# Rounding angles straight from PSUM, with ScalarE emptying the products and taking the absolute value

## The chip, the cores and the metric

The kernel runs on one core of a Trainium2 chip. A core has TensorE (PE in the profile, its weight loads PEld), VectorE (DVE), ScalarE (ACT), GpSimd (POOL) and SyncE (SP, which only issues transfers). The metric is the device time of one launch in microseconds. The kernel before took 1151.37, 1149.21 and 1151.18 us in three runs (median 1151.18).

## The reference

For 8 batches with 8 heads, 576 rows and head size 64, float32: scores scaled by 1/sqrt(64); those more than `tau` = 0.02 under the row's largest are dropped; softmax; product with v. The heads of a batch side by side give x (576 × 512). Then a mixture with trigonometric weights:

```
theta = x @ w_theta
zr, zi = x * cos(theta), x * sin(theta)
y = w_tok_r @ zr + w_tok_i @ zi          (over the 576 rows)
u = x + y
out = u + max(u @ w_ch, 0)
```

The change lies in how cos(theta) and sin(theta) are formed.

## The kernel before, in words

**Attention.** Heads go in pairs, four pairs to a batch, 32 in all. A pair has nine blocks of scores (128 query rows of one head, the last one 64 rows of both). For each: scores on PE into PSUM (L278); L282 on VectorE copies them negated to SBUF and takes the row minimum; L295 adds `tau`; L299 on ScalarE is the exp; L300 on VectorE masks and sums. Four transposes (L326) and a fifth (L341) follow on PE, and ScalarE copies their results to SBUF (L331, L333 for the last block, L344, L348). When the first 256 query columns are there, and again after the other 320, the value product o_ps (L361, 20 matmuls) runs, and L362 on ScalarE copies it out. L377 to L386 normalise.

**The mixture.** `moe(b)` handles batch b while the attention of batch b + 1 runs. Its operands are transposed: 4 chunks m of 128 of the 512 columns, each 128 partitions × 576. For each m:

- *angle*: 24 matmuls give the product in two halves of 288 columns, each in a PSUM buffer (m_ps, L405). The half is emptied into `th` as turns (angle / 2 pi), by ScalarE for m = 0 and 1 (L444), by VectorE for m = 2 and 3 (L446). Adding and subtracting the constant `MAGIC` rounds to whole turns (L453, SBUF to SBUF, into `km`); L454 takes the difference, a fraction between −1/2 and 1/2.
- *sines*, for two m at a time: L463 on VectorE clears the sign bit into the first half of `z`; ScalarE loads the Sin table (L467), makes the cosine from the absolute value (L471) and the sine from the fraction (L472), and loads the Exp table again (L476). GpSimd multiplies both with x (L483); in the last batch VectorE does.
- *flip*: z is transposed (z_ps, L495), copied out in a high part by ScalarE (L497) and a low part by VectorE (L498).
- *token*: 54 matmuls per m (y_ps, L512), added to x by L515. At the end comes the product with w_ch, L560.

**What sets the order.** PE's order is written by hand: `fill()` lets the mixture yield pieces between the blocks of attention, and `ORDER = "a0 a1 s01 a2 a3f0 s23 t0f1 t1f2 t2f3 t3"` sets the mixture's steps (a angle, s sines, f flip, t token). On the other engines a scheduler with its own time model orders the instructions at compile time, by priorities: attention's are raised by `ATTENTION` (20), the sines and the table loads by `SINES` (10000). `after(...)` adds order without a semaphore. So the order on VectorE, ScalarE, GpSimd and SP's queue can change wherever an instruction of the mixture changes.

**Buffers.** Six PSUM buffers (`ps_t`) are shared by m_ps, z_ps, y_ps, t_ps, o_ps and those of normalising; a buffer comes free when all readers of its content are done. Four SBUF buffers (`temp`, tag t576) are shared by `th`, `km`, the reciprocal rows `rb`, and the raw q and k that SP loads (`qraw`, `kraw`) and from which ScalarE and GpSimd prepare the next pair (L100, L109, L225, L226, L228). Three buffers hold `z`.

Of the kernel before, what the change touches and what calls it, by code (L numbers as in the profile page):

```python
# [12 lines left out]
U32 = mybir.dt.uint32  # L13
AF = mybir.ActivationFunctionType
ALU = mybir.AluOpType
# [3 lines left out]
MAGIC = 12582912.0  # L19
TURN = 2.0 * math.pi  # L20

TURN_IN = 6.283185
# [17 lines left out]
def tile_attn_moe(  # L40
# [11 lines left out]
    nc = tc.nc  # L52
    B, NP, D, _, S = qT.shape
# [3 lines left out]
    HS = S // 2  # L57
# [53 lines left out]
    def temp(name, dt=F32):  # L111
        return pool.tile([P, S], dt, tag="t576", name=name, bufs=4)

    def after(ins, other):

        info = mybir.DependencyInfo(mybir.DependencyClass.NoSync, mybir.DependencyReason.DATA)
        tc.add_manual_dep(ins.ins, other.ins.name, info, reason="order")
        return ins
# [71 lines left out]
    def get_wm(which, m):  # L190
        t = pool.tile([P, 2, NM, P], F32R, tag="wm", name=f"wm{which}", bufs=3)
        nc.gpsimd.dma_start(t, wm_dram[which, m].bitcast(F32R))  # L192
        return t
# [234 lines left out]
    def moe(b):  # L428
# [7 lines left out]

        def angle(m):
            th = temp("th")
            wm = get_wm(0, m)

            def evict(ps, hs):

                if m < 2:
                    nc.scalar.activation(out=th[:, hs], in_=ps[:, :HS], func=AF.Copy, scale=1.0 / TURN)  # L444
                else:
                    nc.vector.tensor_scalar(  # L446
                        out=th[:, hs], in0=ps[:, :HS], scalar1=1.0 / TURN, scalar2=None, op0=ALU.mult
                    )

            yield from product(wm, xs, evict, m == 0)  # L450

            km = temp("km")
            nc.vector.tensor_scalar(out=km, in0=th, scalar1=MAGIC, scalar2=-MAGIC, op0=ALU.add, op1=ALU.add)  # L453
            nc.vector.tensor_tensor(out=th, in0=th, in1=km, op=ALU.subtract)  # L454
            zs[m, "f"] = th

        def sines(ms):

            todo = []
            for m in ms:  # L460
                th = zs.pop((m, "f"))
                z = pool.tile([P, 2 * S], F32, tag="z", name="z", bufs=3)
                ab = nc.vector.tensor_scalar(  # L463
                    out=z[:, :S].bitcast(U32), in0=th.bitcast(U32), scalar1=0x7FFFFFFF, scalar2=None, op0=ALU.bitwise_and
                )
                todo.append((m, th, z))
            ahead_of = after(nc.scalar.preload_act_table(AF.Sin), ab)  # L467
            with tc.high_priority(offset=SINES):
                for m, th, z in todo:
                    ins = [  # L470
                        nc.scalar.activation(out=z[:, :S], in_=z[:, :S], func=AF.Sin, scale=-TURN_IN, bias=half_pi),  # L471
                        nc.scalar.activation(out=z[:, S:], in_=th, func=AF.Sin, scale=TURN_IN),  # L472
                    ]
                    for x in ins:
                        after(x, ahead_of)
                exp = nc.scalar.preload_act_table(AF.Exp)  # L476
                for x in ins:
                    after(exp, x)
            for m, th, z in todo:
                x = xT[b * NP + m]  # L480
                for i in range(2):
                    zi = z[:, i * S : i * S + S]
                    lo_eng.tensor_tensor(out=zi, in0=zi, in1=x, op=ALU.mult)  # L483
                zs[m] = z
# [41 lines left out]
        for what in ORDER.split():  # L526
            ms = [int(x) for x in what if x.isdigit()]
            turns = what[2:3] == "f"
            what, m = what[0], ms[0]
            if what == "a":  # L530
                other = flip(ms[1]) if turns else iter(())
                for n, cost in enumerate(angle(m)):
                    yield cost
                    if n > 1:
                        yield next(other, 0)
                for cost in other:
                    yield cost
                left -= 1
            elif what == "s":
                sines(ms)  # L540
            elif what == "f":
                yield from flip(m)
            else:
                other = flip(ms[1]) if turns else iter(())
                for n, cost in enumerate(token(m)):
                    yield cost
                    if n % 5 == 2:
                        yield next(other, 0)
                for cost in other:
                    yield cost  # L550
                done.append(m)
            while left == 0 and done:
                split_u(done.pop(0))
# [146 lines left out]
```

## Time and profile before

| | |
|---|---|
| three runs, us | 1149.21, 1151.18, 1151.37 |
| profiled execution: span, us (the page gives no other time for it) | 1147.4 |
| busy us: PE / PEld | 1043.9 / 921.5 |
| busy us: DVE / ACT / POOL | 869.0 / 750.0 / 375.1 |
| chain that ended last: PE / DVE / ACT | 64% / 15% / 13% |

The profile is that of one execution. A row of groups gives line, engine, operation, output <- inputs, shapes and count, then after the bar the busy time in us and the mean of one in ns, and then the idle time of that engine just before, with what ended it. A row of waits gives engine, tile and line, what it waited for, the sum in us, how often, and the longest. A row of the timeline gives start and duration in us, and in brackets the idle time before it and what ended it; adjacent instructions of one kind are put in one row with their count. A row of windows gives the busy time of each engine in a stretch, then the granted clock of PE as a share of full speed.

### The profile page before, as it was taken

The numbers are of one execution on the slowest core, as the hardware profiler recorded it, in microseconds if no ns is written. First come the engines' busy times: TensorE is split into PE (matmuls) and PEld (weight loads), VectorE is DVE, ScalarE is ACT, GpSimd is POOL, SyncE is SP. The second block draws the span as 40 slices with busy tenths as digits, with TensorE's granted clock in tenths as the row PEclk, the third lists the DMA queues.
The fourth block names the chain that finished last, engine by engine and source line by source line (L and its number), as shares of the span: only waits on it lengthen the run. The fifth ranks groups of instructions, "written<-read, shape, count | busy, mean of one in ns | idle before, by whom it ended". The sixth has DMA issues, their size and how long they took to land.

```text
span 1147.4 us, 21175 instructions
## 1 busy us (share of the span) xinstructions
PE 1043.9 (91%) x7736; PEld 921.5 (80%) x7736; DVE 869.0 (76%) x2139; ACT 750.0 (65%) x1394; POOL 375.1 (33%) x303
## 2 busy tenths in 40 slices
PE   4888888799899998999979998999989999799998
PEld 3566687688779987898869987799878998689898
DVE  7998777987877677876787768776788678787362
ACT  6766869666676566964677666865678656774350
POOL 2203325233342243521443234422435314430210
PEclk9999999999999998999999999999999999999999
DMA  7722223255231052213432142311522133310421
GB/s 252 213 81 84 64 71 97 88 138 148 76 100 53 28 178 74 79 47 103 116 100 63 32 146 76 102 53 34 173 87 72 43 113 104 97 32 1 120 71 60
DMA packets 55176, 105.26 MB, mean 92 GB/s; under 512 B 11936, under 2 KB 20128, under 8 KB 55072
## 3 DMA queue, kind: packets, MB, share of 16 engines
q1 hardware_dynamic: 45856, 70.35, 20.9%
q0 software_dynamic: 9216, 33.56, 10.2%
q8 instruction: 61, 1.00, 0.4%
q14 instruction: 43, 0.35, 0.1%
HBM read 90.24 MB, written 13.63 MB: 91 GB/s over the span
## 4 chain that ended last, share of the span: by engine, by line
PE 64%; DVE 15%; ACT 13%; issue 4%; DMA 2%; POOL 1%; SPq 0%; ACTq 0%; POOLq 0%; DVEq 0%
PE y_ps L512 15%; PE m_ps L405 13%; PE o_ps L361 13%; PE s_ps L278 11%; PE t_ps L326 7%; DVE sc L282 3%; DVE s_sb L300 3%; DVE km L453 3%; ACT s_sb L299 3%; DMA qraw<-in_qT_dram 2%; ACT a L331 2%; PE rb_ps L377 1%; PE z_ps L495 1%; ACT z L471 1%; ACT z L472 1%
## 5 line engine op out<-in xcount | busy, mean ns | idle before, releaser
L300 DVE SCALAR_TENSOR_TENSOR s_sb<-sc,nm,s_sb 128x576 f32<-128x576 f32 x288 | 276.1, 960 | 69.4 <-ACT s_sb L299 65.5
L299 ACT ACTIVATE s_sb<-sc,nm 128x576 f32<-128x576 f32 x288 | 224.1, 778 | 110.8 <-DVE sc L282 109.9
L278 PE MATMUL s_ps<-k,qq 128*128 128x288 f32 (+1 forms) x1344 | 240.2, 307 | 53.8 <-DVE sc L282 39.8
L282 DVE TENSOR_SCALAR_CACHE_REDUCE sc<-s_ps 128x576 f32<-128x576 f32 x288 | 216.7, 753 | 67.2 <-PE s_ps L278 64.3
L278 PEld LDWEIGHTS s_ps<-k,qq 128*128 128x128 f32 x1344 | 193.8, 192 | 81.4 <-DVE sc L282 46.6
L361 PE MATMUL o_ps<-a,v 128*64 128x320 f32 (+1 forms) x1280 | 180.2, 430 | 31.2 <-DVE nm L295 27.7
L331 ACT COPY a<-t_ps 128x512 f32<-128x512 f32 x256 | 148.2, 579 | 58.2 <-PE t_ps L326 56.9
L326 PE MATMUL t_ps<-ident,s_sb 128*128 128x128 f32 x1152 | 175.4, 275 | 1.7 <-DVE zl L498 1.7
L361 PEld LDWEIGHTS o_ps<-a,v 128*64 128x64 f32 x1280 | 92.5, 143 | 97.8 <-ACT s_sb L299 30.4
L512 PE MATMUL y_ps<-wt_h,zh 128*128 128x288 f32 x576 | 165.2, 305 | 6.3 <-DVE zl L498 4.8
L512 PE MATMUL y_ps<-wt_l,zh 128*128 128x288 f32 x576 | 163.0, 301 | 0.0
L109 POOL TENSOR_TENSOR k<-kraw,k 128x576 fp32r<-128x576 f32 x62 | 90.8, 1465 | 202.4 <-ACT k L100 201.0
L228 POOL TENSOR_TENSOR qq<-qraw,qq 64x576 fp32r<-64x576 f32 x62 | 95.1, 1534 | 159.9 <-ACT qq L226 130.4
L326 PEld LDWEIGHTS t_ps<-ident,s_sb 128*128 128x128 f32 x1152 | 142.4, 142 | 3.8 <-DVE zl L498 1.9
L512 PEld LDWEIGHTS y_ps<-wt_h,zh 128*128 128x128 f32 x576 | 108.6, 188 | 8.1 <-DVE zl L498 6.2
L512 PEld LDWEIGHTS y_ps<-wt_l,zh 128*128 128x128 f32 x576 | 108.6, 189 | 0.0
L512 PE MATMUL y_ps<-wt_h,zl 128*128 128x288 f32 x576 | 103.6, 306 | 0.0
L192 POOL DMA_DIRECT2D wm<-wm_dram x64 | 36.4, 570 | 171.0 <-PE m_ps L405 142.6
L405 PE MATMUL m_ps<-xh,wm 128*128 128x288 f32 x512 | 91.5, 305 | 0.3 <-ACT xh L100 0.3
L483 POOL TENSOR_TENSOR z<-z,xT 128x576 f32<-128x576 f32 x56 | 80.0, 1457 | 31.5 <-ACT z L471 31.4
L109 POOL TENSOR_TENSOR ul<-xT,uh 128x576 fp32r<-128x576 f32 x24 | 34.7, 1448 | 169.8 <-DVE uh L104 169.8
L405 PE MATMUL m_ps<-uh,wm 128*128 128x288 f32 x512 | 84.0, 299 | 0.0
(85 smaller groups left out, 1641.9 us busy)
## 6 DMA issues: line engine op xcount, KB each, us to landing
wm<-wm_dram POOLq DMA_DIRECT2D x64, 512.0 KB, 4.0
qraw<-in_qT_dram SPq DMA_DIRECT2D x128, 144.0 KB, 2.9
kraw<-in_kT_dram SPq DMA_DIRECT2D x128, 144.0 KB, 2.9
out_dram<-xT SPq DMA_DIRECT2D x32, 288.0 KB, 2.2
v<-in_vp_dram SPq DMA_DIRECT2D x32, 256.0 KB, 2.7
wraw<-in_w_tok_dram SPq DMA_DIRECT2D x9, 576.0 KB, 5.0
wraw<-in_w_theta_dram SPq DMA_DIRECT2D x4, 512.0 KB, 4.4
wm_dram<-whi SPq DMA_DIRECT2D x8, 256.0 KB, 2.3
```

The lines of the kernel that those rows point to most:

```text
L109: eng_lo.tensor_tensor(out=lo, in0=src, in1=hi.bitcast(F32), op=ALU.subtract)
L228: eng.tensor_tensor(out=qq[64:128], in0=raw[64:128], in1=qq[64:128].bitcast(F32), op=ALU.subtract)
L278: nc.tensor.matmul(ps[:, h, d0:d1], st, kk, start=(x == 0), stop=(x == len(todo) - 1))
L282: nc.vector.tensor_scalar(out=sc.rearrange("p (a b) -> p a b", a=2), in0=ps[:, :, :HS], scalar1=-1.0, scalar2=None, op0=ALU.mult, op1=ALU.min,
L299: nc.scalar.activation(out=e, in_=u.ps[j], func=AF.Exp, bias=nm[:, j : j + 1], scale=-1.0)
L300: nc.vector.scalar_tensor_tensor(out=e, in0=u.ps[j], scalar=nm[:, 2 + j : 3 + j], in1=e, op0=ALU.is_le, op1=ALU.mult, accum_out=u.pr.rows[ ...
L326: nc.tensor.transpose(out=tp[:, c * P : (c + 1) * P], in_=u.sf[:, k0 + c * P : k0 + (c + 1) * P], identity=ident)
L331: nc.scalar.copy(out=t.a[:, :, j, q0 : q0 + P], in_=tp.rearrange("p (c q) -> p c q", c=4))
L361: nc.tensor.matmul(o[64 * j : 64 * j + 64, :w], st, mv, start=(c == 0), stop=(c == 4))
L405: nc.tensor.matmul(tiles[h][:, :HS], wm[:, a, c, :], parts[c][bb][:, hs], start=(count[h] == 0), stop=(count[h] == 11))
L483: lo_eng.tensor_tensor(out=zi, in0=zi, in1=x, op=ALU.mult)
L512: nc.tensor.matmul(ps[:, :HS], z, w, start=(n == 0), stop=(n == len(work) - 1))
```

## The change

All four products are emptied by ScalarE (L444). VectorE no longer rounds from SBUF: it reads each half of the product in PSUM a second time and writes angle / 2 pi + MAGIC into `km` (L445); the constant's subtraction moves into one two-source operation over 576 columns, (km − MAGIC) − th (L451), which gives the negated fraction, so the sine's scale changes its sign. The absolute value becomes an activation (L462). `km` is taken from its pool before the product and not after it. The lines behind move up by three: L464 is the Sin table's load, L468 the cosine, L469 the sine, L473 the Exp table's load, L480 the multiplication with x, L492, L494 and L495 the flip.

```diff
         def angle(m):
             th = temp("th")
+            km = temp("km")
             wm = get_wm(0, m)
 
             def evict(ps, hs):
 
-                if m < 2:
-                    nc.scalar.activation(out=th[:, hs], in_=ps[:, :HS], func=AF.Copy, scale=1.0 / TURN)
-                else:
-                    nc.vector.tensor_scalar(
-                        out=th[:, hs], in0=ps[:, :HS], scalar1=1.0 / TURN, scalar2=None, op0=ALU.mult
-                    )
+                nc.scalar.activation(out=th[:, hs], in_=ps[:, :HS], func=AF.Copy, scale=1.0 / TURN)
+                nc.vector.tensor_scalar(
+                    out=km[:, hs], in0=ps[:, :HS], scalar1=1.0 / TURN, scalar2=MAGIC, op0=ALU.mult, op1=ALU.add
+                )
 
             yield from product(wm, xs, evict, m == 0)
 
-            km = temp("km")
-            nc.vector.tensor_scalar(out=km, in0=th, scalar1=MAGIC, scalar2=-MAGIC, op0=ALU.add, op1=ALU.add)
-            nc.vector.tensor_tensor(out=th, in0=th, in1=km, op=ALU.subtract)
+            nc.vector.scalar_tensor_tensor(
+                out=th, in0=km, scalar=MAGIC, in1=th, op0=ALU.subtract, op1=ALU.subtract
+            )
             zs[m, "f"] = th
...
-                ab = nc.vector.tensor_scalar(
-                    out=z[:, :S].bitcast(U32), in0=th.bitcast(U32), scalar1=0x7FFFFFFF, scalar2=None, op0=ALU.bitwise_and
-                )
+                ab = nc.scalar.activation(out=z[:, :S], in_=th, func=AF.Abs)
...
-                        nc.scalar.activation(out=z[:, S:], in_=th, func=AF.Sin, scale=TURN_IN),
+                        nc.scalar.activation(out=z[:, S:], in_=th, func=AF.Sin, scale=-TURN_IN),
```

PE's order is the same in both programs. The other engines' is not. ScalarE at the first sines (m = 0 and 1) of the second batch's mixture, before: one stretch from the Sin table to the Exp table, then the last value tiles of the pair (L333, L348):

```order
L444 ACTIVATE th<-m_ps 128x288 x2
L299 ACTIVATE s_sb<-sc,nm 128x576
L331 COPY a_3312<-t_ps 128x4x128
L344 COPY a_3313<-t_ps 128x128
L467 ACT_TABLE_LOAD
L471 ACTIVATE z<-z,small 128x576
L472 ACTIVATE z<-th 128x576 x2
L471 ACTIVATE z<-z,small 128x576
L476 ACT_TABLE_LOAD
L333 COPY a_3312<-t_ps 128x8x64
L348 COPY a_3313<-t_ps 64x64 x2
L299 ACTIVATE s_sb<-sc,nm 128x576 x2
```

The same place now:

```order
L462 ACTIVATE z<-th 128x576
L464 ACT_TABLE_LOAD
L468 ACTIVATE z<-z,small 128x576
L469 ACTIVATE z<-th 128x576 x2
L444 ACTIVATE th<-m_ps 128x288 x2
L299 ACT_TABLE_LOAD
L299 ACTIVATE s_sb<-sc,nm 128x576
L333 COPY a_3318<-t_ps 128x8x64
L468 ACT_TABLE_LOAD
L468 ACTIVATE z<-z,small 128x576
L473 ACT_TABLE_LOAD
L348 COPY a_3319<-t_ps 64x64 x2
```

The absolute value stands ahead of the Sin table; two evictions of m = 2, an exp with its own table load and L333 have moved in among the sines, and the second cosine, with a load on either side, stands ahead of L348.

VectorE there, before, from the last absolute value of the first sines on (L446 are the two halves of m = 2, L453 its rounding):

```order
L463 TENSOR_SCALAR z<-th 128x576
L446 TENSOR_SCALAR th<-m_ps 128x288
L282 TENSOR_SCALAR sc,nm<-s_ps 128x576
L446 TENSOR_SCALAR th<-m_ps 128x288
L295 TENSOR_SCALAR nm<-nm,small 128x1
L453 TENSOR_SCALAR km<-th 128x576
L282 TENSOR_SCALAR sc,nm<-s_ps 128x576
L454 TENSOR_TENSOR th<-th,km 128x576
L446 TENSOR_SCALAR th<-m_ps 128x288
```

and now:

```order
L300 SCALAR_TENSOR_TENSOR s_sb,rows_3400<-sc,nm,s_sb 128x576
L451 SCALAR_TENSOR_TENSOR th<-km,th 128x576
L282 TENSOR_SCALAR sc,nm<-s_ps 128x576
L295 TENSOR_SCALAR nm<-nm,small 128x1
L282 TENSOR_SCALAR sc,nm<-s_ps 128x576
L295 TENSOR_SCALAR nm<-nm,small 128x1
L445 TENSOR_SCALAR km<-m_ps 128x288 x2
L451 SCALAR_TENSOR_TENSOR th<-km,th 128x576
```

The second L282, which stood behind L453, is now ahead of the roundings of m = 2.

ScalarE at the second sines (m = 2 and 3) of the same batch, before:

```order
L467 ACT_TABLE_LOAD
L471 ACTIVATE z<-z,small 128x576
L472 ACTIVATE z<-th 128x576 x2
L331 COPY a_3545<-t_ps 128x4x128
L344 COPY a_3546<-t_ps 128x128
L299 ACT_TABLE_LOAD
L299 ACTIVATE s_sb<-sc,nm 128x576
L471 ACT_TABLE_LOAD
L471 ACTIVATE z<-z,small 128x576
L476 ACT_TABLE_LOAD
```

and now:

```order
L462 ACTIVATE z<-th 128x576
L464 ACT_TABLE_LOAD
L468 ACTIVATE z<-z,small 128x576
L469 ACTIVATE z<-th 128x576 x2
L468 ACTIVATE z<-z,small 128x576
L473 ACT_TABLE_LOAD
L331 COPY a_3554<-t_ps 128x4x128
L344 COPY a_3555<-t_ps 128x128
L299 ACTIVATE s_sb<-sc,nm 128x576
```

L331, which the second value product of the next pair needs, stands behind all four sines and the Exp table. GpSimd has one addition for q (L228) that stood ahead of the second sines' four multiplications with x with its partner; now the partner stands behind them and one k addition.

## The prediction

> **What bounds the kernel now.** I read the page first: busy shares, then the chain that ended last.
>
> ```profile
> span 1147.4 us, 21175 instructions
> PE 1043.9 (91%) x7736; PEld 921.5 (80%) x7736; DVE 869.0 (76%) x2139; ACT 750.0 (65%) x1394; POOL 375.1 (33%) x303
> PE 64%; DVE 15%; ACT 13%; issue 4%; DMA 2%; POOL 1%; SPq 0%; ACTq 0%; POOLq 0%; DVEq 0%
> ```
>
> TensorE (PE) bounds the kernel as a whole: it is idle for only 1147.4 − 1043.9 = 103.5 us, and no edit of this change touches a matmul. Whatever the change is worth must therefore come out of, or be added to, the places where PE waits. So the waits come next, then the groups of the lines that change.
>
> ```profile
> PEld o_ps L361 <- ACT s_sb L299: 30.4, 20, 4.7
> PE o_ps L361 <- DVE nm L295: 27.7, 7, 4.5
> ```
>
> ```profile
> L453 DVE TENSOR_SCALAR km<-th 128x576 f32<-128x576 f32 x32 | 45.4, 1420 | 6.9 <-ACT th L444 6.3
> L454 DVE TENSOR_TENSOR th<-th,km 128x576 f32<-128x576 f32 x32 | 31.2, 974 | 0.6
> L463 DVE TENSOR_SCALAR z<-th 128x576 uint32<-128x576 uint32 x32 | 22.5, 704 | 0.3
> L472 ACT ACTIVATE z<-th 128x576 f32<-128x576 f32 x32 | 19.9, 669 | 0.0
> ```
>
> Seven times, up to 4.5 us each, PE stands before the value matmuls (o_ps); and rounding (L453) averages 1420 ns. The shapes of these groups are single, so that mean hides something. The timeline of the second batch's mixture shows it (start, duration):
>
> ```profile
> 305.05 0.46 DVE L463 TENSOR_SCALAR z<-th 128x576 uint32<-128x576 uint32 x1
> 306.71 5.51 POOL L483 TENSOR_TENSOR z<-z,xT 128x576 f32<-128x576 f32 x4
> 307.10 5.44 DVE L453 TENSOR_SCALAR km<-th 128x576 f32<-128x576 f32 x1
> 308.33 1.28 ACT L476 ACT_TABLE_LOAD   x1
> 309.62 0.59 ACT L333 COPY a<-t_ps 128x512 f32<-128x512 f32 x1
> 312.46 0.74 DVE L282 TENSOR_SCALAR_CACHE_REDUCE sc<-s_ps 128x576 f32<-128x576 f32 x1
> 313.81 0.44 DVE L446 TENSOR_SCALAR th<-m_ps 128x288 f32<-128x288 f32 x1
> 314.40 4.00 PE L361 MATMUL o_ps<-a,v 128*64 128x320 f32 x14 [4.47 <-DVE nm L295]
> 316.56 3.39 PE L361 MATMUL o_ps<-a,v 128*64 128x320 f32 x12
> 320.01 0.43 ACT L362 COPY xT<-o_ps 128x320 f32<-128x320 f32 x1 [1.72 <-PE o_ps L361]
> 332.87 2.38 PE L361 MATMUL o_ps<-a,v 128*64 128x256 f32 x20 [0.50 <-DVE xT L515]
> ```
>
> An operation that takes 0.46 us elsewhere lasts from 307.10 to 312.54, to just after POOL's four multiplies end at 312.22. The score eviction L282 and the product eviction L446 stand behind it on VectorE; L446 frees the PSUM buffer that o_ps needs. Then the granted clock falls:
>
> ```profile
> core 0: us, PE busy (x) PEld busy (x) DVE busy (x) ACT busy (x) POOL busy (x), PEclk, DMA share, GB/s
> 312.40:320.50 8.10, 6.10 (x26) 3.06 (x27) 4.42 (x12) 3.11 (x6) 0.00 (x0) 0.58 0.19 50
> ```
>
> What this site costs is read by comparing batches, from the long L453 to the second o_ps of the same batch (256 columns):
>
> ```profile
> 169.65 1.23 DVE L453 TENSOR_SCALAR km<-th 128x576 f32<-128x576 f32 x1
> 173.28 2.91 PE L361 MATMUL o_ps<-a,v 128*64 128x320 f32 x20 [0.80 <-DVE nm L295]
> 187.61 2.52 PE L361 MATMUL o_ps<-a,v 128*64 128x256 f32 x20 [0.38 <-DVE xT L515]
> 709.03 5.45 DVE L453 TENSOR_SCALAR km<-th 128x576 f32<-128x576 f32 x1
> 716.35 4.27 PE L361 MATMUL o_ps<-a,v 128*64 128x320 f32 x20 [4.49 <-DVE nm L295]
> 721.42 0.41 ACT L362 COPY xT<-o_ps 128x320 f32<-128x320 f32 x1
> 733.82 2.38 PE L361 MATMUL o_ps<-a,v 128*64 128x256 f32 x20 [0.50 <-DVE xT L515]
> 974.58 5.44 DVE L453 TENSOR_SCALAR km<-th 128x576 f32<-128x576 f32 x1
> 999.42 1.95 PE L361 MATMUL o_ps<-a,v 128*64 128x256 f32 x16 [0.50 <-DVE xT L515]
> ```
>
> In the first batch (no lock-out) that distance is 17.96; in the six after it 25.77, 25.51, 24.49, 24.79, 24.58 and 24.84. All seven add up to 167.94. If every batch were like the first, 167.94 − 7 × 17.96 = 42.2 us would be gained. That is the prize. The eighth batch multiplies on VectorE and has no such stall.
>
> **The change part by part.**
>
> *VectorE, removed.* L453 (45.4), L454 (31.2), L463 (22.5) and the evictions L446:
>
> ```profile
> L446 DVE TENSOR_SCALAR th<-m_ps x32: 437/449/458, 168.0 to 1099.9; 128x288 f32<-128x288 f32 x32
> L444 ACT ACTIVATE th<-m_ps x32: 407/412/422, 154.4 to 1090.8; 128x288 f32<-128x288 f32 x32
> L300 DVE SCALAR_TENSOR_TENSOR s_sb<-sc,nm,s_sb x288: 801/819/2030, 13.1 to 1067.3; 128x576 f32<-128x576 f32 x144
> ```
>
> (min/median/max ns). That is 14.4 for 32 L446, 113.5 us together. *Added:* 64 roundings from PSUM (L445). No row has this pair of operations; the nearest is L446, the same engine, source and size: 449, so 64 × 0.45 = 28.8. Its maximum over 32 runs is 458, where L454 beside it goes to 1930, so it was not locked out; I take that for L445. From the other side, a rounding that can be locked out costs up to L453's 5.44. And 32 two-source operations (L451): between L454's median 759 and L300's mean 960, so 24 to 31. VectorE thus loses 54 to 61 us of busy time, 30 of them the lock-out (45.4 − 32 × 0.46 = 30.7).
>
> The skill's rule on L445: the Trainium skill, VectorE: DVE Perf Modes, "Why PSUM operands drop a tier", says that the two-port mode needs both SBUF read ports, which a PSUM operand excludes. By it L445 cannot be locked out; L446's 458 ns maximum agrees, and the sum is the same.
>
> *ScalarE, added.* 32 more evictions at 0.412 = 13.2, and 32 absolute values. No row has Abs; two L444 make 0.82 for its columns, L472 takes 0.669 at the same engine, size and buffers. I take L472, 21.4 in all: 35 us more. Table loads stay at 47, but they move.
>
> *Waits added.* The two readers of a product tile are put in sequence: each L445 waits for ScalarE's L444 of the same half, and only then is the PSUM buffer free. Behind a waiting L445 stand L295, L300 and the next L282 on VectorE; for L295 waits the exp, for L300 the transposes. Where ScalarE is late, VectorE and PE are now late too.
>
> *First sines (the site above).* In the order, ScalarE's run there has four table loads instead of two, and the Abs and two product evictions in between, all ahead of the first value tile. I replay it on the clock of the second batch. The fraction is ready at about 305.4, when L463 ended before (305.5): L445 comes earlier than the old rounding, but L300 stands ahead of L451. Then Abs to 306.1; table 307.4; three sines at the 0.62 pitch to 309.3:
>
> ```profile
> 302.06 0.71 ACT L444 ACTIVATE th<-m_ps 128x288 f32<-128x288 f32 x2
> 306.40 1.24 ACT L472 ACTIVATE z<-th 128x576 f32<-128x576 f32 x2
> 310.10 0.42 ACT L348 COPY a<-t_ps 64x64 f32<-64x64 f32 x2
> 310.55 0.77 ACT L299 ACTIVATE s_sb<-sc,nm 128x576 f32<-128x576 f32 x1
> ```
>
> two evictions (0.71 for two) 309.95; Exp table 311.25; exp 312.0; L333 to 312.5. Before, the table load ran ahead of VectorE's absolute value, and L333 came at 309.62. So o_ps starts at 312.6, not 314.40. But only 16 of its 20 matmuls can: the last four wait for L348, behind Sin table (313.8), one cosine (314.6), Exp table (315.85) and L348 (316.25). End of o_ps: 316.9, against 319.95 before in this batch, and 318.69 in the fifth (716.35 + 4.27, less 709.03 − 307.10 = 401.93).
>
> This lead of 1.8 to 3.0 us is mostly lost at once. L362, which normalising waits for, now stands behind L348, an exp, L331, L444, a z copy and another Abs: 316.25 + 0.78 + 0.57 + 0.41 + 0.59 + 0.67 = 319.3, against 721.42 − 401.93 = 319.5 in the fifth batch. PE's wait is cut in pieces of at most 1.6 us, since the z transposes now wait too, for an L445; so I expect no fall of the clock there.
>
> *Second sines.* From the scores that follow (ending, by the replay, at 322.3; in a typical batch before, 322.6) one chain leads on: L282, L495, L445, L295 (0.76 + 0.69 + 0.45 + 0.20) to 324.4; L451, beside POOL's q addition, about 1.0; Abs 326.1; Sin table 327.4; four sines 329.9 to 330.4; Exp table 331.7; L331 332.2. Before, L331 went ahead of the last cosine and the second table:
>
> ```profile
> 330.21 0.56 ACT L331 COPY a<-t_ps 128x512 f32<-128x512 f32 x1
> ```
>
> So the second o_ps starts at 332.3, 25.2 after 307.1: ScalarE's chain gives back the whole prize. The table load that goes there (two instead of four) does not help, since it lay behind L331.
>
> *Sum.* Seven batches at 25.2 are 176.4, 8.5 more than 167.94; nearly all of it is the first batch, 7.2. There some 2 us come back, because three short waits of PE right after it are filled anyway (0.38 is one of them, above): 6.5. In the last batch the chain evict, rounding, two-source, Abs, table, sine is longer by the Abs and an eviction behind a table, 1.3 to 2: I take 1.5. Together +8 on the profiled 1147.4, a span of 1155.4. The page gives no other time for that execution; the three runs (1149.21 to 1151.37, median 1151.18) lie 3.8 above it, so **1159 us**.
>
> *Moved.* The rounding buffer is taken before the product, so one q load goes later in SP's queue, and POOL's k and q preparation of the next pair stands behind four multiplies; its margin is about 1 us by the replay. Cost 0; without the cover, below.
>
> A rule that would make it worse: the Trainium skill, ScalarE: Activation LUTs, "What ACT_TABLE_LOAD costs", gives 1283 ns and a drain of about 1380 ns for each switch. By it the two more loads on the path would cost 2 × 7 × 1.38 = 19 us more (an estimate). The trace has the duration (1.28) but no drain: the load at 308.33 ends at 309.61, and L333 starts at 309.62. I go by the trace.
>
> **The rivals.**
>
> *The stall goes and nothing replaces it.* For it: VectorE's queue is what PE waited for (27.7 us), and the ScalarE replay stacks estimates; if the evictions or Abs issue earlier, o_ps comes earlier. All of it: 1151.2 − 42.2 = 1109; half: 1130. Against: the four table loads in one run (5.1 us) are in ScalarE's order. 0.08 and 0.20.
>
> *No difference.* Needs a mean distance of 24.0, that is 1.2 us per batch less than I have: an Abs and an eviction. 1149 to 1153.5; 0.12.
>
> *The next pair's scores come late.* POOL's multiplies come in a run of 4 × 1.39 = 5.5 us; k and q preparation behind them, 1 us margin. If it fails by 2 us on seven batches: 1159 + 14 = 1173. It decides from the point where the q addition (L228) lands after PE is through with the y matmuls. Against: the replay's margin. 0.10.
>
> *The lock-out stays.* L451 reads two SBUF tiles beside the same multiplies. If it waits for three of them (4.2 us), the Abs and L300 behind it are late by 3 us in seven batches: 1180. Against: L300 and L454, also two-source, were never longer than 2.03 and 1.93:
>
> ```profile
> L454 DVE TENSOR_TENSOR th<-th,km x32: 742/759/1930, 156.9 to 1101.8; 128x576 f32<-128x576 f32 x32
> ```
>
> 0.05. The Trainium skill, SBUF — State Buffer, "Who interferes with whom", states a rule for this: such a VectorE instruction contends with a GpSimd one that reads SBUF, and the loser fully blocks. The trace agrees up to one POOL multiply (1.4), not beyond.
>
> **How the numbers follow.** My forecast has 0.45; with the rivals 0.28, 0.12, 0.10 and 0.05. About 0.2% (2.3 us) is what a measurement here tells from no change. Slower: 0.45 + 0.10 + 0.05 = 0.60; same 0.12; faster 0.28. The likeliest case's own range is 1151 to 1168 (1.2 us per batch either way: a POOL multiply met or missed at its end). The range to hold 8 in 10 takes in the half-gain and the smaller late cases: 1132 to 1172.
>
> **What would show it.** L445 within 0.43 to 0.47 always; no VectorE group with members over 2.1 us; the wait of o_ps on VectorE gone, and in its place waits of PE on ScalarE (L333, L348, L331), each below 2 us; clock 1.00 through the site; the distance to the second o_ps near 25 in all seven batches, the first included. I am wrong if ScalarE idles in the site, if the distance falls to 18 to 22, or if PE waits for POOL's q addition.

## The result, and the profile after

The changed kernel takes 1163.33 us (median; 1159.75 to 1167.64) against 1150.89 (1149.21 to 1151.37): a ratio of 1.0102, 95% interval 1.0081 to 1.0124. It is slower, by 12 us (1.0%) at the medians; the forecast was 8. The profiled executions differ by 14.7 us of span. From the page after:

```profile
span 1162.1 us, 21225 instructions
PE 1052.4 (91%) x7736; PEld 919.1 (79%) x7736; DVE 834.7 (72%) x2107; ACT 778.2 (67%) x1458; POOL 383.5 (33%) x303
PE 56%; ACT 18%; DVE 17%; issue 4%; DMA 3%; POOL 1%; SPq 0%; ACTq 0%; DVEq 0%; POOLq 0%
```

VectorE lost 34 us of busy time (869.0 to 834.7), ScalarE gained 28, and ScalarE's share of the chain that ended last went from 13% to 18%. The new operations cost what was reckoned (the first three rows give ns min/median/max; the last two are L300's group, after and before):

```profile
L445 DVE TENSOR_SCALAR km<-m_ps x64: 446/457/459, 155.6 to 1114.8; 128x288 f32<-128x288 f32 x64
L451 DVE SCALAR_TENSOR_TENSOR th<-km,th x32: 748/758/1929, 157.5 to 1116.0; 128x576 f32<-128x576 f32 x32
L462 ACT ACTIVATE z<-th x32: 677/686/708, 158.3 to 1117.0; 128x576 f32<-128x576 f32 x32
L300 DVE SCALAR_TENSOR_TENSOR s_sb<-sc,nm,s_sb 128x576 f32<-128x576 f32 x288 | 279.6, 971 | 113.4 <-ACT s_sb L299 107.5
L300 DVE SCALAR_TENSOR_TENSOR s_sb<-sc,nm,s_sb 128x576 f32<-128x576 f32 x288 | 276.1, 960 | 69.4 <-ACT s_sb L299 65.5
```

The three new groups are busy for 28.4, 32.5 and 22.1 us. VectorE's net 34 us is still less than the 54 to 61 forecast. Two groups that the change does not touch became longer (L366 from 5.4 to 10.9 us, L300 by 3.5), and VectorE's instructions overlap less now: added up one by one they lost 41 us. L445 is never over 459 ns, so the lock-out of the rounding is gone; two of them ran at 316.05 and 316.42 beside a multiply of POOL (316.03 to 317.43) and took 0.46 and 0.45 us. But VectorE now idles 107.5 us ahead of L300, for the exp on ScalarE; before it was 65.5. PE's waits around the value product moved from VectorE to ScalarE:

```profile
PE o_ps L361 <- ACT a L331: 12.5, 7, 1.8
PE z_ps L492 <- DVE km L445: 8.9, 7, 1.3
PE o_ps L361 <- ACT a L333: 7.8, 7, 1.1
PE o_ps L361 <- ACT a L348: 7.3, 5, 1.5
```

Before, one row stood there: 27.7 us, seven times, on VectorE. Now there are four, 36.5 us together: three wait for copies on ScalarE, and the z transposes for L445, which itself idled 16.5 us for the evictions L444 on ScalarE. The timeline of the second batch's mixture, a stretch that opens 6.44 us later than before (the two L444 at 308.50, before at 302.06):

```profile
308.50 0.71 ACT L444 ACTIVATE th<-m_ps 128x288 f32<-128x288 f32 x2
311.80 0.69 ACT L462 ACTIVATE z<-th 128x576 f32<-128x576 f32 x1 [0.96 <-DVE th L451]
312.50 1.28 ACT L464 ACT_TABLE_LOAD   x1
315.63 0.69 ACT L444 ACTIVATE th<-m_ps 128x288 f32<-128x288 f32 x2
316.33 1.28 ACT L299 ACT_TABLE_LOAD   x1
318.31 0.57 ACT L333 COPY a<-t_ps 128x512 f32<-128x512 f32 x1
318.89 1.28 ACT L468 ACT_TABLE_LOAD   x1
318.93 2.37 PE L361 MATMUL o_ps<-a,v 128*64 128x320 f32 x16 [1.11 <-ACT a L333]
322.28 0.43 ACT L348 COPY a<-t_ps 64x64 f32<-64x64 f32 x2
322.75 0.76 PE L361 MATMUL o_ps<-a,v 128*64 128x320 f32 x4 [1.45 <-ACT a L348]
325.36 0.44 ACT L362 COPY xT<-o_ps 128x320 f32<-128x320 f32 x1
338.02 0.59 ACT L331 COPY a<-t_ps 128x512 f32<-128x512 f32 x1
338.66 2.37 PE L361 MATMUL o_ps<-a,v 128*64 128x256 f32 x18 [1.80 <-ACT a L331]
```

Less 6.44: absolute value at 305.36 (replayed 305.4), the 16 matmuls at 312.49 (312.6), L348 at 315.84 (its start was put at 315.85), L362 at 318.92 (319.3), the second o_ps at 332.22 (332.3). ScalarE's queue is what PE waits for.

Where the 14.7 us of span came from, batch by batch: the start of L362 for the first value product of each batch's last pair, after minus before, is 0.65, 6.00, 6.02, 5.66, 7.43, 7.76, 9.15 and 11.23. So 0.65 comes ahead of the first mixture; the mixtures add 5.35, 0.02, −0.36, 1.77, 0.33, 1.39 and 2.08; the last batch 3.5. Counted by PE, only 6.2 of the 14.7 us are more idle time (103.5 to 109.7); its busy time rose by 8.5 for the same matmuls. So the rows of waits say where the order hurts, but do not add up to the whole loss.

### The profile page after: what moved, and what is told of

The parts are those of the page before. It is cut to its first block, busy times and chain, and to the rows that moved or that the text cites. A ratio compares the mean times of both kernels' runs of the same rounds, so it can differ in the third digit from the quotient of the medians.

```text
span 1162.1 us, 21225 instructions
## 1 busy us (share of the span) xinstructions
PE 1052.4 (91%) x7736; PEld 919.1 (79%) x7736; DVE 834.7 (72%) x2107; ACT 778.2 (67%) x1458; POOL 383.5 (33%) x303
## 4 chain that ended last, share of the span: by engine, by line
PE 56%; ACT 18%; DVE 17%; issue 4%; DMA 3%; POOL 1%; SPq 0%; ACTq 0%; DVEq 0%; POOLq 0%
PE y_ps L509 14%; PE o_ps L361 12%; PE m_ps L405 10%; PE s_ps L278 10%; PE t_ps L326 6%; DVE sc L282 4%; DVE s_sb L300 4%; ACT s_sb L299 3%; DMA qraw<-in_qT_dram 3%; ACT z L468 2%; ACT L464 2%; PE z_ps L492 2%; ACT L473 1%; DVE th L451 1%; ACT z L469 1%
## 5 line engine op out<-in xcount | busy, mean ns | idle before, releaser
L300 DVE SCALAR_TENSOR_TENSOR s_sb<-sc,nm,s_sb 128x576 f32<-128x576 f32 x288 | 279.6, 971 | 113.4 <-ACT s_sb L299 107.5
L282 DVE TENSOR_SCALAR_CACHE_REDUCE sc<-s_ps 128x576 f32<-128x576 f32 x288 | 217.0, 753 | 84.6 <-PE s_ps L278 81.1
L331 ACT COPY a<-t_ps 128x512 f32<-128x512 f32 x256 | 148.5, 580 | 55.9 <-PE t_ps L326 54.0
L361 PEld LDWEIGHTS o_ps<-a,v 128*64 128x64 f32 x1280 | 89.4, 140 | 100.2 <-ACT a L331 15.7
L109 POOL TENSOR_TENSOR k<-kraw,k 128x576 fp32r<-128x576 f32 x62 | 94.3, 1520 | 206.8 <-ACT k L100 205.2
L228 POOL TENSOR_TENSOR qq<-qraw,qq 64x576 fp32r<-64x576 f32 x62 | 98.2, 1584 | 101.9 <-ACT qq L226 68.4
L480 POOL TENSOR_TENSOR z<-z,xT 128x576 f32<-128x576 f32 x56 | 81.0, 1472 | 56.5 <-ACT z L468 56.5
```

Of the source, the lines that this page charges most:

```text
L109: eng_lo.tensor_tensor(out=lo, in0=src, in1=hi.bitcast(F32), op=ALU.subtract)
L228: eng.tensor_tensor(out=qq[64:128], in0=raw[64:128], in1=qq[64:128].bitcast(F32), op=ALU.subtract)
L282: nc.vector.tensor_scalar(out=sc.rearrange("p (a b) -> p a b", a=2), in0=ps[:, :, :HS], scalar1=-1.0, scalar2=None, op0=ALU.mult, op1=ALU.min,
L300: nc.vector.scalar_tensor_tensor(out=e, in0=u.ps[j], scalar=nm[:, 2 + j : 3 + j], in1=e, op0=ALU.is_le, op1=ALU.mult, accum_out=u.pr.rows[ ...
L331: nc.scalar.copy(out=t.a[:, :, j, q0 : q0 + P], in_=tp.rearrange("p (c q) -> p c q", c=4))
L361: nc.tensor.matmul(o[64 * j : 64 * j + 64, :w], st, mv, start=(c == 0), stop=(c == 4))
```

## The experiments

Two theories stood against each other at first, and a third beside them. A: ScalarE's stand-in for the removed stall, that is the order on ScalarE at the two places of the sines. B: each PSUM half is read twice in sequence. C: the earlier rounding buffer. D came later: 35 us more work on ScalarE cost time wherever they stand. In all of these, "before" and "changed" are the two kernels above; each ratio is to the kernel before, run again beside that experiment (medians 1151.81 to 1152.39). A table at the end of this section sets the runs side by side.

**The absolute value back on VectorE.**

```diff
-                ab = nc.scalar.activation(out=z[:, :S], in_=th, func=AF.Abs)
+                ab = nc.vector.tensor_scalar(
+                    out=z[:, :S].bitcast(U32), in0=th.bitcast(U32), scalar1=0x7FFFFFFF, scalar2=None, op0=ALU.bitwise_and
+                )
```

> The changed kernel with the absolute value back on VectorE (sign bit cleared, SBUF to SBUF); evictions and rounding as changed. Theory A (ScalarE's stand-in: the lock-out of VectorE is gone, but the absolute value, the two product evictions and two more table loads stand ahead of the value tiles L333, L348 and L331 on ScalarE, and spend the gain): ScalarE loses 0.69 per absolute value, L348 now comes ahead of the second Sin load (2 us earlier at the first sines), but the second sines now have four loads as well, so part comes back: 1145 to 1157, against 1163. Theory B (the serial reading of each PSUM half, L445 behind L444, is what costs): unchanged, 1160 to 1166. Theory C (the rounding buffer taken earlier moves the q load and the k and q preparation): unchanged, 1160 to 1166.

Measured 1162.19, ratio to before 1.0077 (1.0051 to 1.0102): no better than the changed kernel. A's number missed; B and C had forecast it. The scheduler's answer to the edit was 61 table loads instead of 47, and o_ps still waited for L333; after that wait the granted clock was 0.79 (over 320 to 328 us), and its 20 matmuls took 4.60 us instead of 2.91:

```profile
321.42 0.56 ACT L333 COPY a<-t_ps 128x512 f32<-128x512 f32 x1
322.04 4.60 PE L361 MATMUL o_ps<-a,v 128*64 128x320 f32 x20 [1.27 <-ACT a L333]
```

The 14 more table loads of 1.28 us took the place of the absolute values: ScalarE is busy for 777.1 us, in the changed kernel for 778.2. So this run does not show what less work on ScalarE would be worth, and it does not yet exclude B and C.

**The rounding from PSUM alone.** Evictions of m = 2 and 3 and absolute values on VectorE, as before.

```diff
+                if m < 2:
+                    nc.scalar.activation(out=th[:, hs], in_=ps[:, :HS], func=AF.Copy, scale=1.0 / TURN)
+                else:
+                    nc.vector.tensor_scalar(
+                        out=th[:, hs], in0=ps[:, :HS], scalar1=1.0 / TURN, scalar2=None, op0=ALU.mult
+                    )
-                nc.scalar.activation(out=th[:, hs], in_=ps[:, :HS], func=AF.Copy, scale=1.0 / TURN)
...
-                ab = nc.scalar.activation(out=z[:, :S], in_=th, func=AF.Abs)
+                ab = nc.vector.tensor_scalar(
+                    out=z[:, :S].bitcast(U32), in0=th.bitcast(U32), scalar1=0x7FFFFFFF, scalar2=None, op0=ALU.bitwise_and
+                )
```

> Of the change only the rounding from PSUM with the two-source fraction: the products of m = 2 and 3 are emptied by VectorE and the absolute value is made on VectorE, as before. Theory A: no lock-out (every rounding under 0.47 us), and ScalarE carries neither evictions for m = 2, 3 nor absolute values; L333 at 310.2 on the clock of the second batch instead of 312.5, L348 right behind it: some 5 us per batch less than the changed kernel at the first sines, 2 at the second: 1115 to 1135, well below the kernel before (1151). Theory B: half the products are still read twice in sequence, across engines: 1155. Theory C: the buffer is taken early here too: 1160 or more.

Measured 1134.68, ratio 0.9838 (0.9802 to 0.9874). VectorE has more to do than in the changed kernel (855.6 us busy), the rounding is as quick, and the waits of o_ps are all but gone (the z transposes wait 7.4 us for L331):

```profile
L450 DVE TENSOR_SCALAR km<-m_ps x64: 445/448/460, 155.1 to 1085.2; 128x288 f32<-128x288 f32 x64
PE o_ps L361 <- ACT a L331: 1.9, 7, 0.3
PE o_ps L361 <- DVE xT L519: 1.1, 7, 0.2
```

So the part of the change that ends the lock-out is a gain of 1.6%. C expected 1160 or more here, since the buffer is taken early too: C is out as a cause of the loss. B is out for the half of the products that ScalarE empties, but not for the rest.

**The evictions back on VectorE, the absolute value on ScalarE.** Of the diff above only the part on the evictions.

> The changed kernel with the products of m = 2 and 3 emptied by VectorE again; absolute value on ScalarE as changed. Theory A: two evictions (0.71) less on ScalarE ahead of L333, but the absolute value stays, and L348 stays behind the second Sin load: about 1 us per batch less than the changed kernel, 1150 to 1158. Theory B: the reads of m = 2 and 3 no longer cross engines, most of the loss goes: 1140. Theory C: unchanged, 1160 to 1166.

Measured 1166.87, ratio 1.0104 (1.0057 to 1.0152). B expected 1140: B is out. A's 1150 to 1158 was missed as well. C's 1160 to 1166 is near, but the rounding alone, which takes the buffer early too, had ruled C out. The waits name the same places, with L331 at the second sines the largest:

```profile
PE o_ps L361 <- ACT a L331: 18.6, 7, 2.9
PE o_ps L361 <- ACT a L348: 10.1, 7, 1.4
PE o_ps L361 <- ACT a L333: 7.2, 7, 1.0
```

**The four sines kept together.** Every operation of the changed kernel stays; the order among the sines and the loads is what changes. The first version has m in reverse.

```diff
-            ahead_of = after(nc.scalar.preload_act_table(AF.Sin), ab)
+            ahead_of = None
...
-                for m, th, z in todo:
+                for m, th, z in todo[::-1]:
...
-                        after(x, ahead_of)
+                        if ahead_of is not None:
+                            after(x, ahead_of)
+                        ahead_of = x
```

> The changed kernel, every operation the same, but the four sines of a pair of m are kept together: the Sin table is loaded only once the absolute values are ready, in front of the first of four activations in a fixed order. 33 table loads instead of 47; L333 and L331 come ahead of the Sin table. Theory A: at the first sines o_ps ends some 2.4 us earlier than in the changed kernel, at the second L331 no longer waits for two loads and four sines, 3 to 4 us; seven batches: 1163 - 40 = 1123 (1115 to 1135). Theory B and theory C: reads and buffers are as in the changed kernel, so 1158 to 1165.

Measured 1175.93, ratio 1.0197 (1.0153 to 1.024): the wrong way. No wait on L331, L333 or L348 is left, but a new one took their place:

```profile
PE z_ps L494 <- POOL z L482: 39.9, 7, 5.7
```

PE's order transposes the z of m = 0 first, and the reversed sines made it last. That was a fault of the edit, so it was made again with m = 0 (or 2) in front. To keep the four together, the first cosine waits for the last absolute value.

```diff
-            ahead_of = after(nc.scalar.preload_act_table(AF.Sin), ab)
+            ahead_of = ab
+            cls = mybir.DependencyClass.Sync
...
-                        after(x, ahead_of)
+                        after(x, ahead_of, cls)
+                        ahead_of, cls = x, mybir.DependencyClass.NoSync
```

> The changed kernel once more with its four sines kept together behind one Sin load, but in their old order (m = 0 or 2 first). In the run before this one the reversed order made PE wait 5.7 us in each of seven batches for the product of x with the z of m = 0 (39.9 us in all). Theory A (ScalarE's order, not its operations): that wait falls to 1 to 2 us, L333 and L331 keep their places ahead of the Sin table, so each batch ends 2.5 to 4 us earlier than in the changed kernel: 1135 to 1148, at or below the kernel before. Theory D (35 us of added work on ScalarE cost time wherever they stand): 1158 to 1166.

Measured 1137.24, ratio 0.9873 (0.9854 to 0.9892): 26 us under the changed kernel with the same arithmetic on the same engines, and 1.3% under the kernel before. The time is in A's range, and far under D's and under the 1158 to 1165 that B and C gave a grouped kernel; the products are still read twice across engines, and the buffer is still taken early. ScalarE carries the absolute values and all evictions as before, but 14 table loads (18 us) are gone, and its busy time is 756.9 us instead of 778.2. That the order counts and not this amount is seen beside the reversed run: there ScalarE is busy for 757.9 us, and the time is 1175.93. In the second batch L333 now stands ahead of the Sin table, and o_ps starts without a wait for ScalarE; what is left of a wait is for z (the 4.23 us of o_ps, at a granted clock of 0.79 over 313 to 321 us, belong to this batch; in the six others it is 2.91):

```profile
310.55 0.58 ACT L333 COPY a<-t_ps 128x512 f32<-128x512 f32 x1
311.15 1.28 ACT L469 ACT_TABLE_LOAD   x1
314.76 0.66 PE L494 MATMUL z_ps<-ident,z 128*128 128x128 f32 x4 [2.46 <-POOL z L482]
316.17 4.23 PE L361 MATMUL o_ps<-a,v 128*64 128x320 f32 x20
```

and the waits of the whole run:

```profile
PE z_ps L494 <- POOL z L482: 17.2, 7, 2.5
PE s_ps L278 <- POOL k L109: 13.8, 14, 1.4
```

The second row is the rival of the prediction on the next pair's scores: POOL's k additions behind its four multiplies. In the changed kernel no such wait of PE showed; ScalarE was later still.

**Rounding alone, sines together.** The two edits above joined.

> Rounding from PSUM alone (evictions of m = 2, 3 and absolute values on VectorE), which ran at 1134.7, with the four sines kept together in their old order: 33 table loads. Theory A: two loads (2.6 us) less at the first sines, of which PE sees one or two per batch, since L348 already stood ahead of the second Sin load: 1122 to 1133. If the loads were hidden anyway: 1132 to 1138.

Measured 1147.76, ratio 0.9961 (0.9949 to 0.9973): 13 us more than without grouping, and above both ranges expected. z_ps waits 15.6 us for POOL, o_ps 7.3 for L331, which in this order stands behind the second group. Keeping the sines together is not good by itself. The waits point at which attention copy is put behind them, and at how late z is.

**The kernel before, sines together.**

> The kernel before with nothing but the order of its sines changed: four together behind one Sin load. Before, the first sines had two loads anyway, and the two more at the second stood behind L331. Theory A: the lock-out of VectorE by POOL's four multiplies stays (a rounding of 5.4 us in six batches), and L331 now stands behind four sines and the second load at the second sines, 1.9 us: 1150 to 1165. If grouping by itself were what made the changed kernel's order good: 1125 to 1140.

Measured 1149.53, ratio 0.9979 (0.9967 to 0.9992). That is just under A's range, but the expectation had read the order wrongly: L331 stands ahead of the Sin load of the second sines here too. The lock-out stays (longest rounding 5458 ns), and so does its wait:

```profile
L453 DVE TENSOR_SCALAR km<-th x32: 452/460/5458, 158.6 to 1106.0; 128x576 f32<-128x576 f32 x32
PE o_ps L361 <- DVE th L446: 28.7, 7, 4.6
```

So keeping the sines together is worth 0.2% in the kernel before, 2.3% in the changed kernel, and loses 1.2% with the rounding alone: the worth of an order depends on what else the kernel leaves to wait for.

**The rounding as a two-source operation in the kernel before.**

```diff
-            nc.vector.tensor_scalar(out=km, in0=th, scalar1=MAGIC, scalar2=-MAGIC, op0=ALU.add, op1=ALU.add)
+            nc.vector.scalar_tensor_tensor(out=km, in0=th, scalar=MAGIC, in1=less, op0=ALU.add, op1=ALU.add)
```

(`less` is a tile that holds −MAGIC.)

> The kernel before with one operation replaced: the rounding reads th and a tile that holds -MAGIC, both in SBUF (scalar_tensor_tensor), instead of th and two constants. Evictions, difference and absolute values as before; SBUF to SBUF, and beside the same four multiplies of POOL. Theory A1 (only the form with one tile is locked out for the whole run of POOL's multiplies; a form with two tiles waits at most for the multiply under way): the rounding is 0.75 to 2.1 us everywhere, the wait of 4.5 us before o_ps goes; but the scheduler gives this kernel 61 table loads instead of 47, so 1135 to 1155. Rival A2 (anything of VectorE's that reads SBUF is held off by POOL's run): the rounding still reaches 5 us, and the time is 1151 or more.

Measured 1140.36, ratio 0.9889 (0.9865 to 0.9913), within A1's range. But the reason is not A1's. The rounding still reaches 3.06 us, and it ends after POOL's whole run:

```profile
310.53 4.17 POOL L485 TENSOR_TENSOR z<-z,xT 128x576 f32<-128x576 f32 x3
312.26 3.06 DVE L455 SCALAR_TENSOR_TENSOR km<-th,less 128x576 f32<-128x576 f32 x1
PE o_ps L363 <- DVE th L448: 13.1, 7, 2.1
```

The run ends at 314.70, the rounding at 315.32; a multiply ended at 313.34, and VectorE did not get in there. That is what A2 said, on a shorter run. The fourth multiply came later, because the scheduler gave this kernel a second Sin load at the first sines; that shortened the lock-out, and o_ps waited 13.1 us for VectorE, 2.1 at most, where it had been 27.7 and 4.5.

**No evictions.** The split of w_theta scales by 1 / (2 pi), so the product is in turns, and both operations of a half read PSUM. One run with VectorE's absolute value, one with ScalarE's; sines together.

```diff
-                nc.scalar.activation(out=th[:, hs], in_=ps[:, :HS], func=AF.Copy, scale=1.0 / TURN)
-                nc.vector.tensor_scalar(
-                    out=km[:, hs], in0=ps[:, :HS], scalar1=1.0 / TURN, scalar2=MAGIC, op0=ALU.mult, op1=ALU.add
-                )
+                nc.vector.tensor_scalar(out=km[:, hs], in0=ps[:, :HS], scalar1=MAGIC, scalar2=None, op0=ALU.add)
+                nc.vector.scalar_tensor_tensor(
+                    out=th[:, hs], in0=km[:, hs], scalar=MAGIC, in1=ps[:, :HS], op0=ALU.subtract, op1=ALU.subtract
+                )
```

> No eviction at all: w_theta is scaled by 1 / (2 pi) when it is split, so that the products are turns; VectorE adds the rounding constant to each half in PSUM, and a two-source operation, one source in SBUF and one in PSUM, makes the fraction of the half. Absolute values on VectorE, four sines kept together. ScalarE then has 32 evictions less than the kernel before, and VectorE 113.5 - (64 x 0.45 + 64 x 0.45 + 14.5) = 41 us less. Theory A: as the run with rounding alone and grouped sines, less some 0.4 us per eviction that stood ahead of L333 or L362: 1115 to 1130. Theory D: the same, 1115 to 1130.

> No evictions (the weights carry 1 / (2 pi)), absolute value on ScalarE, four sines together. Against the run with VectorE's absolute values (1137.2): there VectorE's 32 absolute values took 789 ns on the mean, that is they were held off beside POOL, and L331's and L333's counterparts made PE wait 25 us since the sines come early. ScalarE's absolute value takes 0.69 without that: 1128 to 1138.

Measured 1137.23 (0.9862; 0.9834 to 0.9891) and 1142.5 (0.9914; 0.9896 to 0.9932). ScalarE has the least work of all here (719.8 us busy in the first), and yet both missed what was expected (1115 to 1130, and 1128 to 1138), and neither is faster than the rounding alone (0.9802 to 0.9874, which the first can't be told from). The sines come early, and L337 and L339 (the L331 and L333 of this kernel) stand behind them:

```profile
PE o_ps L367 <- ACT a L337: 13.8, 7, 2.8
PE o_ps L367 <- ACT a L339: 11.7, 7, 1.7
```

Less work, later copies, and no gain: against D once more.

**Buffers of its own for the rounding.** On the kernel with sines together (1137.24).

```diff
-            km = temp("km")
+            km = pool.tile([P, S], F32, tag="km", name="km", bufs=2)
```

> As the changed kernel with its four sines together in their old order (1137.2), and the rounding buffer from two buffers of its own instead of the four that it shares with the raw q and k. The order then has one k addition and both q additions on POOL ahead of the four multiplies of the second sines, as in the kernel before. In the run without this PE waited 13.8 us for such k additions, up to 1.4 us fourteen times. Theory C in its small form (the earlier buffer costs nothing in the changed kernel, where ScalarE is later still, but up to 13 us once that is mended): 1124 to 1134. If those waits only hide behind others: 1135 to 1139.

Measured 1163.63, ratio 1.0103 (1.0088 to 1.0119). Both ranges expected are missed. The waits for k went, but the scheduler moved L331 behind the second sines again, and 18 matmuls took 4.45 us after it instead of 2.37, at a granted clock of 0.69 (over 333 to 344 us). At the same place, in six batches, o_ps waits for VectorE as well, for the addition of y to x (L514 here):

```profile
337.21 0.58 ACT L331 COPY a<-t_ps 128x512 f32<-128x512 f32 x1
337.84 4.45 PE L361 MATMUL o_ps<-a,v 128*64 128x256 f32 x18 [2.60 <-ACT a L331]
PE o_ps L361 <- DVE xT L514: 10.5, 6, 2.8
```

C in its small form can't be told apart in this run. The operations are those of the kernel with sines together, ScalarE is busy for 757.9 us against 756.9, and the time is 1164 instead of 1137: the order that came with the buffers does that, not more work. Which part of it L331's place has (15.6 us of waits in six batches) and which part the waits for L514 have was not taken apart.

**The evictions on VectorE, sines together.**

> As the changed kernel with its four sines together (1137.2), but with the products of m = 2 and 3 emptied by VectorE. The two evictions (0.71) that stand ahead of the Sin load go; PE's wait for POOL's z product (17.2 in seven batches, 2.5 each) should fall by 0.7 each, VectorE has room: 1130 to 1137. Theory D (ScalarE's added work costs wherever it stands) expects more, 13 us of work less: 1124 to 1130.

Measured 1130.92, ratio 0.9826 (0.9796 to 0.9855): the lowest median of all, and 1.7% under the kernel before; its interval overlaps that of the rounding alone (0.9802 to 0.9874), so the two are not told apart. z_ps waits 13.3 us for POOL instead of 17.2, that is 0.56 per batch against the 0.7 expected:

```profile
PE z_ps L499 <- POOL z L487: 13.3, 7, 1.9
```

The runs side by side. "Shift" is the change against before of the L362 mentioned above, from the last pair of the first mixture to that of the seventh, six batches later:

| kernel | us | table loads | L331 at the second sines | shift over six batches, us |
|---|---|---|---|---|
| before | 1150.9 to 1152.4 | 47 | behind three sines | 0 |
| changed | 1163.3 | 47 | behind | +5.2 |
| absolute value on VectorE | 1162.2 | 61 | behind three sines | +3.0 |
| evictions on VectorE | 1166.9 | 47 | behind | 0.0 |
| rounding alone | 1134.7 | 47 | behind, its Sin load early | −19.2 |
| together, reversed | 1175.9 | 33 | ahead | +13.2 |
| together | 1137.2 | 33 | ahead | −20.2 |
| together, evictions on VectorE | 1130.9 | 33 | ahead | −24.2 |
| no evictions, absolute value on VectorE, together | 1137.2 | 33 | behind | −20.6 |
| no evictions, absolute value on ScalarE, together | 1142.5 | 33 | behind | −15.2 |
| together, own buffers | 1163.6 | 33 | behind | +5.8 |
| together, before | 1149.5 | 33 | ahead | +2.3 |
| together, rounding alone | 1147.8 | 33 | behind | −9.6 |
| two-source rounding | 1140.4 | 61 | behind three sines | −13.9 |

The place of L331 alone does not sort these times: with the rounding alone it stands behind the second sines, but PE waits only 1.9 us for it in all.

## Why the prediction was right, and where it was not

*The lock-out.* Right. L445 is 446 to 459 ns in all 64 cases; the kernel with only this part of the change gains 18 us (1152.39 to 1134.68), and grouping without it gains 3. The whole prize of 42 us was never won: the best kernel has 21 (1152.15 to 1130.92).

*ScalarE at the first and second sines.* Right, to within 0.4 us at each step of the replay shown above. Whether the order or the operations cost the time the prediction left open; it counted the absolute value, the evictions and the loads alike. The experiments settle that for the order, on ScalarE and with it on the other engines: three kernels with the same operations and 757 to 758 us of work on ScalarE take 1137, 1164 and 1176 us.

*The distance to the second o_ps* was put at 25.2 in every batch. In the second it is 338.66 − 6.44 − 307.10 = 25.12. The first batch was to lose 7.2, of which some 2 were to come back: 5.2, and the list above has 5.35. All seven together were to lose 6.5 and lost 10.6 (11.23 − 0.65). The fourth and the seventh make up 2.8 of the difference of 4.1, the second and the sixth 0.6 and 0.8; for these two no cause was found.

*The clock.* Wrong in two batches: "I expect no fall of the clock there". In five batches it stays at 1.00; in the fourth and the seventh it falls at both sites, after waits no longer than in the others. At the first sines of the fourth batch it is about half for some 3.4 us, yet o_ps lasts 4.59 us from its first matmul to its last, as in the other batches (4.58), since the slower matmuls only fill the wait for L348. At the second o_ps, for which the prediction has no word on the clock, it costs time. The windows are the first site of the fourth batch, then the second o_ps of the second and of the fourth:

```profile
core 0: us, PE busy (x) PEld busy (x) DVE busy (x) ACT busy (x) POOL busy (x), PEclk, DMA share, GB/s
586.70:590.30 3.60, 3.25 (x14) 1.53 (x16) 1.35 (x2) 3.55 (x4) 1.86 (x2) 0.53 0.00 0
587.05 4.59 PE L361 MATMUL o_ps<-a,v 128*64 128x320 f32 x20 [1.11 <-ACT a L333]
335.00:343.00 8.00, 5.98 (x44) 4.32 (x43) 3.95 (x10) 7.97 (x15) 6.45 (x5) 1.00 0.23 68
603.00:611.00 8.00, 5.99 (x31) 3.34 (x29) 3.50 (x9) 7.78 (x15) 6.31 (x5) 0.79 0.25 72
606.79 4.06 PE L361 MATMUL o_ps<-a,v 128*64 128x256 f32 x18 [1.78 <-ACT a L331]
```

18 matmuls take 4.06 us at a clock of 0.79 over the window, against 2.37: 1.7 us in each of the two batches. It is part of why the fourth and the seventh add 1.77 and 2.08 to the list above, where 0.71 and 0.36 were forecast.

*The last batch.* Under-sized: 1.5 was taken. The first y matmul of that batch starts at 1112.82 against 1098.79, 14.03 late, and 11.23 were brought along: 2.8. By the end it is 3.5.

*The sum.* Forecast 8, measured 12.4 at the medians and 14.7 in the profiled pair. In the other runs the time is about 1.8 above the span of the same execution, so the profiled 1147.4 belongs to the fastest run (1149.21); the 3.8 that the prediction put on to reach the median are 2 of spread, and that is most of the difference between 14.7 and 12.4. Of the 6.7 missing in the pair, the mixtures have 4.1 (two falls of the clock among them), the last batch 2.0, and 0.65 came ahead of the first mixture, where the prediction looked for nothing. The mechanism was right; the size of the sum was low by a third at the medians.

*The k and q preparation, at 0.* Right for the changed kernel. With the sines together 13.8 us of waits for k showed; what they cost was not measured, since the run without them got another order.

*Two-source operations "never longer than 2.03 and 1.93".* This was used against the rival that the lock-out stays. L451 kept to it (1929), but the reason given does not hold in general: the same form reached 3.06 in six batches of the kernel before with only the rounding replaced.

## What to carry to other kernels

Where a scheduler sets the order on an engine, work that is moved to that engine can cost by what it puts behind it, more than by what it takes: the arithmetic of the changed kernel gave 1163 us in the scheduler's order and 1137 in another. So read, for each engine that gets work, which instruction of the critical stage is queued behind it, and if it must not be, order that by hand. A change of several parts is best taken apart: here the rounding from PSUM alone is a gain of 1.6%, and either companion added to it turned that into a loss in the order that the scheduler gave it, though not in every order (the absolute value on ScalarE is part of the kernel with 1130.9).

## What the runs showed of the hardware that was not expected

A rounding with two SBUF sources was held off until the end of POOL's run, over the rest of one multiply and the whole of the next (312.26 to 315.32, the run to 314.70), and in the changed kernel the two-source L451 got in ahead of a waiting multiply:

```profile
314.66 4.65 POOL L480 TENSOR_TENSOR z<-z,xT 128x576 f32<-128x576 f32 x3 [1.54 <-ACT z L468]
316.91 1.14 DVE L451 SCALAR_TENSOR_TENSOR th<-km,th 128x576 f32<-128x576 f32 x1
317.40 1.92 POOL L480 TENSOR_TENSOR z<-z,xT 128x576 f32<-128x576 f32 x1
```

There the third multiply takes 1.92 instead of 1.4. The Trainium skill, SBUF — State Buffer, "Who interferes with whom", says that a VectorE instruction with two SBUF inputs contends with a GpSimd instruction that reads SBUF, and that the shared port pair is an exclusive lock. The trace agrees that one of the two waits. It also shows a hold-off past the end of a multiply (313.34), and what decides which engine comes next was not settled by these runs.

The granted clock fell in two batches of seven, after waits of PE of 1.1 us (first site) and 1.8 us (second), with the same waits in the other five leaving it at 1.00. The clock records of this trace offer a reason that no run tested. The stretches at half clock last 3.41 us, and their starts lie whole multiples of 3.41 us apart (224.95, 586.77, 607.25, 989.54, 1010.02). Cut into such stretches from 200 to 1080 us, the five that end in a fall are those in which PE was busy least (0.31 to 0.41 of the time; 0.48 and more in all others). So it may be where a wait falls on this grid that counts. No exact limit follows: with the sines together 0.49 was followed by a fall, and 0.45 was not.
